# Sparse attention followed by an MLP on one core: two pairs of heads interleaved over all 128 partitions in each load of q or k

## The chip, the cores and the metric

One core of a Trainium2 chip runs the whole kernel. The metric is device time in microseconds (us); a kernel's figure is the median of its runs. Ratios are the mean time of one kernel's fast runs over that of the other's fast runs of the same rounds, so they are not quite the ratio of the medians quoted beside them. Jobs ran on different chips (the last two on the same one), so across jobs I compare the ratios to the kernel before, which ran in every job.

PE is TensorE's matmul side, DVE is VectorE, ACT is ScalarE, POOL is GpSimd, SP is the queue that issues most transfers. PSUM is the memory that PE writes its results to. "The rings", a word of the record, means here the DMA engines taken together.

## The reference

```python
batch, n_heads, seq, head_dim = 8, 8, 576, 64
scores = scale * np.matmul(q, k.transpose(0, 1, 3, 2))
mask_local = (rel >= 0) & (rel < 32)                   # heads 0 to 3
mask_strided = (rel >= 0) & (pos_k % 32 == pos_q % 32) # heads 4 to 7
attn = softmax(np.where(mask, scores, -1e9))           # cut
x = np.matmul(attn, v)                                 # -> (4608, 512)
h = x @ w_in                                           # (512, 2048)
g = np.maximum(h, 0) + alpha * np.minimum(h, 0)
return g @ w_out                                       # (2048, 512)
```

## The kernel before

Attention works on pairs of heads; two pairs of one kind (local or strided) of one batch make a half batch. A half batch is loaded, cast to fp16, transposed on PE through PSUM into `qpad` and `kT`, scored in blocks, masked, multiplied with v, and turned into columns of `xT`. The MLP runs in chunks of 512 tokens: lin1 (`hps`) and lin2 (`ops`). The first chunk, lin1(0), needs batch 0's attention; lin1(1) follows batch 1's and the first steps of batch 2's.

The loads of q and k: q on partitions 0 to 63, k on 64 to 127.

```python
st = spool.tile([128, 2304], F32, tag="qk", name="stqk")
for src, r0 in ((q, 0), (k, 64)):
    keep((k_eng if r0 and k_eng else nc.sync).dma_start(
        st[r0 : r0 + 64, 0:2048].rearrange("p (h e) -> p h e", h=4),
        src[b, h0 : h0 + 4, 0:512, :].rearrange("h (p t) d -> p h (t d)", t=8)))
# ... two more transfers for tokens 512 to 575 (the tail); v local in five, v strided in two
```

A transpose then holds q and k of one pair, and DVE copies out of PSUM:

```python
for t in range(8):
    keep(nc.tensor.transpose(tp[:, t, :], src[:, P.pr, 128 * t : 128 * t + 128], ident))
keep(nc.tensor.transpose(tt[:, 0:128], src[:, P.pr, 1024:1152], ident))
# ... ACT copies kT, DVE copies qpad, one head at a time
```

The start, in the parts that the argument touches:

```python
cast_part(0, False, "v", 0, "pool")
load_w(0, False)                     # w_in, a quarter; issued by POOL, cast on the way
cast_part(0, False, "v", 1, "pool")
load_w(1, False); load_w(2, False); load_w(3, False)   # three lines in the source
# ... batch 0's attention; SP then reads a few elements of w_in ("gate"), which holds
#     batch 1's loads back until the first half of w_in is there
for m in range(16):
    lin1_piece(0, m, True)
    if m == 8:
        # ... casts of batch 1's local part on POOL, loads of batch 2's
        for c in range(4):
            load_w(c, True)          # w_out
    attn_n(0 if m < 12 else 1, end1)
```

The softmax here doesn't subtract the row's maximum and nothing guards it: scores larger than these inputs give would overflow.

## Time and profile before

| | before |
|---|---|
| time, median of 4 runs | 370.15 us |
| lin1(0) starts | 35.5 us |
| lin1(1) starts | 84.9 us |
| rest, lin1(1) to the end | 281.4 us, PE idle 5.4 |

The prediction prints the slices, the table of stages, the chain through the hole and two stretches of the loads, and says how each is read. The rate at which loads came in is on the page too, in the same 40 slices of 9.2 us:

```profile
GB/s 158 207 148 236 235 210 198 209 210 204 215 218 222 137 168 136 135 139 155 97 161 114 167 115 30 30 30 30 30 30 30 29 59 29 29 57 32 29 59 86
```

From the second slice to the 13th it lies between 198 and 236, but for the third (148), in which POOL had not issued most of the weights yet (46 GB/s from 22 to 24 us).

### The profile page before, as it was taken

The page shows a single profiled execution, that of the slowest core. Times are in us where ns is not written, and L with a number is a line of the kernel's source. Part 1 is how long each engine was busy: PE and PEld are TensorE (multiplying, and loading weights), DVE is VectorE, ACT ScalarE, POOL GpSimd, SP SyncE. Part 2 cuts the span into 40 slices and gives each one's busy share as a digit, 9 for nine tenths or more (in the row PEclk, how much of TensorE's full clock was granted, in tenths as well). Part 3 has the DMA queues.
Part 4 walks back from the last instruction along what each step waited for, and adds up shares of the span by engine and source line. Part 5 has one row for each costly group of instructions (what it writes and reads, how often), then busy time and mean ns, then how long its engine had stood idle before and what let it go on. Part 6 is the DMA issues. An engine that isn't in the chain of part 4 may idle for free.

```text
span 366.5 us, 6531 instructions
## 1 busy us (share of the span) xinstructions
PE 330.8 (90%) x2449; PEld 185.4 (51%) x2449; DVE 219.4 (60%) x487; ACT 182.4 (50%) x360; POOL 137.7 (38%) x174
## 2 busy tenths in 40 slices
PE   5837985708999899999999999999999999999996
PEld 1525444604555455555557777555555444444444
DVE  2658589905886167757775776677667444444410
ACT  1614565504755355666665666566665444443421
POOL 2260482155478266546554654565242000000000
PEclk9876799556999999999999999999999999999999
DMA  7999999999999665567384740000000010010012
GB/s 158 207 148 236 235 210 198 209 210 204 215 218 222 137 168 136 135 139 155 97 161 114 167 115 30 30 30 30 30 30 30 29 59 29 29 57 32 29 59 86
DMA packets 54944, 44.11 MB, mean 120 GB/s; under 512 B 35696, under 2 KB 40192, under 8 KB 54912
## 3 DMA queue, kind: packets, MB, share of 16 engines
q1 hardware_dynamic: 49504, 37.24, 46.1%
q0 software_dynamic: 4512, 5.24, 8.0%
q10 hardware_dynamic: 896, 1.21, 1.7%
q8 instruction: 19, 0.31, 0.4%
q14 instruction: 13, 0.11, 0.1%
HBM read 38.43 MB, written 9.44 MB: 131 GB/s over the span
## 4 chain that ended last, share of the span: by engine, by line
PE 75%; DMA 12%; SPq 8%; POOL 2%; ACT 1%; issue 1%; DVE 0%; POOLq 0%; ACTq 0%
PE ops L456 33%; PE hps L411 31%; DMA stv<-in_v_dram 9%; SPq L130 5%; PE sp L229 3%; PE pv L258 3%; PE tp L202 3%; DMA stqk<-in_k_dram 2%; PE xp L275 2%; DMA win<-in_moe_w_in_dram 1%; SPq L103 1%; SPq L107 1%; PE ops L447 1%; ACT osb L461 1%; POOL qk L145 1%
## 5 line engine op out<-in xcount | busy, mean ns | idle before, releaser
L411 PE MATMUL hps<-xT,win 128*128 128x512 f16 (+1 forms) x640 | 148.9, 365 | 0.0
L456 PE MATMUL ops<-wout,gT 128*128 128x512 f16 x560 | 141.4, 379 | 2.0 <-ACT osb L461 2.0
L424 DVE SCALAR_TENSOR_TENSOR gT<-neg,oma,hps 128x512 f16<-128x512 f32 x144 | 106.9, 743 | 59.3 <-ACT neg L421 57.0
L421 ACT ACTIVATE neg<-hps 128x512 f32<-128x512 f32 x144 | 86.0, 597 | 83.0 <-PE hps L411 81.3
L411 PEld LDWEIGHTS <-win 128*128 128x128 f16 x640 | 60.5, 99 | 49.1 <-issue 5.5
L244 POOL TENSOR_TENSOR et<-et,masks 128x384 f16<-128x384 f16 (+2 forms) x60 | 54.4, 908 | 81.5 <-ACT et L237 80.5
L456 PEld LDWEIGHTS <-gT 128*128 128x128 f16 x560 | 50.0, 98 | 49.0 <-issue 2.8
L237 ACT ACTIVATE et<-sp 128x384 f16<-128x384 f32 (+2 forms) x96 | 45.6, 491 | 29.9 <-PE sp L229 29.9
L145 POOL CAST qk<-stqk 128x1024 f16<-128x1024 f32 (+1 forms) x44 | 34.3, 817 | 32.3 <-DMA stqk<-in_k_dram 32.3
L267 DVE TENSOR_TENSOR x<-pv,rc 72x384 f16<-72x384 f32 (+2 forms) x80 | 42.2, 527 | 2.8
L258 PEld LDWEIGHTS <-et 72*128 72x128 f16 (+1 forms) x448 | 24.8, 100 | 28.0 <-POOL et L240 8.1
L265 DVE RECIPROCAL rc<-pv 72x6 f32<-72x6 f32 (+2 forms) x80 | 14.9, 186 | 38.1 <-PE pv L258 37.8
L229 PE MATMUL sp<-qpad,kT 128*128 128x144 f16 (+1 forms) x224 | 32.6, 244 | 4.9 <-DVE qpad L212 2.4
L229 PEld LDWEIGHTS <-kT 128*128 128x128 f16 x224 | 20.6, 101 | 22.9 <-issue 3.5
L461 ACT COPY osb<-ops 128x512 f32<-128x512 f32 x35 | 20.5, 585 | 18.5 <-PE ops L456 18.3
L212 DVE COPY qpad<-tp 64x512 f16<-64x512 f16 x32 | 22.0, 688 | 7.3 <-ACT kT L212 7.1
L202 PE MATMUL tp<-ident,qk 128*128 128x128 f16 x256 | 21.6, 233 | 3.3 <-DVE qk L143 3.0
L202 PEld LDWEIGHTS <-qk 128*128 128x128 f16 x256 | 18.1, 105 | 10.1 <-DVE qk L143 3.9
L258 PE MATMUL pv<-vl,et 128*128 128x65 f16 x192 | 12.2, 195 | 11.8 <-POOL et L240 7.8
L209 DVE COPY qpad<-tp 64x512 f16<-64x512 f16 x32 | 13.5, 421 | 13.7 <-ACT kT L209 13.5
L209 ACT COPY kT<-tp 128x512 f16<-128x512 f16 x16 | 9.3, 583 | 19.3 <-PE tp L202 19.0
L258 PE MATMUL pv<-vs,et 72*128 72x65 f16 x256 | 16.6, 198 | 2.3 <-ACT et L237 1.1
(42 smaller groups left out, 179.2 us busy)
## 6 DMA issues: line engine op xcount, KB each, us to landing
out_dram<-osb SPq DMA_DIRECT2D x35, 256.0 KB, 2.0
stqk<-in_q_dram SPq DMA_DIRECT2D x16, 512.0 KB, 6.3
stqk<-in_k_dram SPq DMA_DIRECT2D x12, 512.0 KB, 7.8
stv<-in_v_dram SPq DMA_DIRECT2D x32, 160.0 KB, 4.4
stv<-in_v_dram SPq DMA_DIRECT2D x8, 512.0 KB, 5.5
win<-in_moe_w_in_dram POOLq DMA_DIRECT2D x4, 512.0 KB, 6.7
wout<-in_moe_w_out_dram POOLq DMA_DIRECT2D x4, 512.0 KB, 16.5
stqk<-in_k_dram ACTq DMA_DIRECT2D x2, 512.0 KB, 7.9
```

Of the source, the lines that this page charges most:

```text
L145: keep(nc.gpsimd.tensor_copy(o, i))
L202: keep(nc.tensor.transpose(tp[:, t, :], src[:, P.pr, 128 * t : 128 * t + 128], ident))
L229: keep(nc.tensor.matmul(sp[:, 2 * w * x : 2 * w * x + 2 * w], P.kT[:, k0 : k0 + 128], P.qpad[:, :, w * t : w * t + w], start=(x == 0), sto ...
L237: keep(nc.scalar.activation(et[0:r, 0:n], sp[0:r, 0:n], AF.Exp, scale=SCALE))
L244: keep(eng.tensor_tensor(ev, ev, m.unsqueeze(1).to_broadcast([r, n // w, w]), op=ALU.mult))
L258: keep(nc.tensor.matmul(pv[:, 65 * x : 65 * x + 65], et[0:r, c : c + 128], v16[0:r, t, 2 * P.pr + hh, :], start=(x == 0), stop=(x == nb - ...
L267: keep(nc.vector.tensor_tensor(P.x16[0:w, c0 : c0 + 64 * nb].rearrange("r (c e) -> r c e", e=64), pvv[:, :, 0:64], rc[0:w, 0:nb].unsqueeze ...
L411: keep(nc.tensor.matmul(hps[:, dst : dst + w], win16[:, kk, 128 * m : 128 * m + 128], xT[:, kk, src : src + w], start=(kk == 0 and x == 0) ...
L421: keep(nc.scalar.activation(neg, hps, AF.Relu, scale=-1.0))
L424: keep(nc.vector.scalar_tensor_tensor(gTs[n][:, m, :], neg, oma[:, m : m + 1], hps, op0=ALU.mult, op1=ALU.add))
L456: keep(nc.tensor.matmul(ops, gTs[n][:, kf, 128 * mt : 128 * mt + 128], wout16[:, kf, :], start=(kf == 0), stop=(kf == 15)))
L461: keep(nc.scalar.copy(osb, ops))
```

## The change

Its intent is to make each load of q and of k span all 128 partitions, to halve the number of transfers, and to keep PE's work the same. Partition 2p+a holds token group p of pair a, so one transpose serves both pairs and its output has the pairs interleaved. With it, `qpad` and `kT` go from three buffers of one pair to two buffers of two pairs.

```diff
-        st = spool.tile([128, 2304], F32, tag="qk", name="stqk")
+        for nm, src, eng in (("q", q, nc.sync), ("k", k, k_eng or nc.sync)):
+            st = spool.tile([128, 2, 512], F32, tag="qk", bufs=6, name=f"st{nm}")
+            base = src[b, h0 : h0 + 1, 0:1, :]
+            keep(eng.dma_start(st, bass.AP(
+                tensor=base.tensor, offset=base.offset,
+                ap=[[8 * D, 64], [2 * S * D, 2], [S * D, 2], [1, 8 * D]])))
... tails of all eight heads in two transfers per batch; v local in one, v strided in one
-    def transpose_piece(P):
+    def transpose_piece(u, nm):
+        tp = pspool.tile([128, 8, 64, 2], F16, tag="ps", name="tp")
+        for t in range(8):
+            keep(nc.tensor.transpose(
+                tp[:, t].rearrange("r p e -> r (p e)"), src[:, 128 * t : 128 * t + 128], ident))
+        main = tp.rearrange("r t p e -> r e t p" if strided else "r t p e -> r e p t")
+        if nm == "q":
+            for hh in range(2):
+                rr = slice(64 * hh, 64 * hh + 64)
+                keep(nc.vector.tensor_copy(split(qpads[u % 2][rr, :, hh, :])[0], main[rr]))
+            return
... k: two tail transposes, two copies on ACT; then the tails of q on DVE
... masks and identity in one load; the small identity of the alpha transpose no longer loaded:
         if i == 13:
+            keep(nc.vector.tensor_copy(id16, ident[0:16, 0:16]))
             keep(nc.tensor.transpose(apt[:, 0:16], alpha_r, id16))
```

More of the change, by code (lines that the diff above doesn't have):

```diff
@@ L13, with _build_consts @@
 AF = mybir.ActivationFunctionType
-def _build_masks():
+def _build_consts():
     kp = np.arange(128)[:, None]
     qf = np.arange(96)[None, :]
-    first = ((qf >= kp) & (qf < kp + 32)).astype(np.float16)
     other = ((qf + 32 >= kp) & (qf < kp)).astype(np.float16)
+    first = np.where(kp < 32, np.float16(0), other)
     ks = np.arange(128)[:, None]
@@ L26, in _build_masks @@
     mstr = ((ks % 4 == qs % 4) & (ks <= qs)).astype(np.float16)
-    return np.concatenate([first, first, other, other, mstr], axis=1)
+    ident = np.eye(128, dtype=np.float16)
+    return np.concatenate([ident, first, first, other, other, mstr], axis=1)
 @with_exitstack
@@ L49 @@
     RING = 4 * S
-    masks_dram = nc.inline_tensor(_build_masks(), name="masks").ap()
-    id_dram = nc.inline_tensor(np.eye(128, dtype=np.float16), name="ident128").ap()
-    id16_dram = nc.inline_tensor(np.eye(16, dtype=np.float32), name="ident16").ap()
+    consts_dram = nc.inline_tensor(_build_consts(), name="consts").ap()
     cpool = ctx.enter_context(tc.tile_pool(name="const", bufs=1))
     spool = ctx.enter_context(tc.tile_pool(name="stage", bufs=3))
+    tpool = ctx.enter_context(tc.tile_pool(name="tl", bufs=2))
     hpool = ctx.enter_context(tc.tile_pool(name="half", bufs=2))
@@ L72 @@
     ))
-    ident = cpool.tile([128, 128], F16)
+    consts = cpool.tile([128, 584], F16)
     id16 = cpool.tile([16, 16], F32)
-    masks = cpool.tile([128, 456], F16)
     alpha_r = cpool.tile([16, 128], F32)
     oma = cpool.tile([128, 16], F32)
-    mfirst, mother, mstr = masks[:, 0:384], masks[:, 192:288], masks[0:72, 384:456]
+    ident = consts[:, 0:128]
+    mfirst, mother, mstr = consts[:, 128:512], consts[:, 320:416], consts[0:72, 512:584]
     win16 = cpool.tile([128, 4, 2048], F16)
@@ L84 @@
     NE = 8
-    qpads = [cpool.tile([128, 2, S], F16, name=f"qpad{i}") for i in range(3)]
-    kTs = [cpool.tile([128, 640], F16, name=f"kT{i}") for i in range(3)]
+    qpads = [cpool.tile([128, 2, 2, S], F16, name=f"qpad{i}") for i in range(2)]
+    kTs = [cpool.tile([128, 2, 672], F16, name=f"kT{i}") for i in range(2)]
     vls = [cpool.tile([128, 6, 4, 65], F16, name=f"vl{i}") for i in range(2)]
@@ L89, with load_tail @@
     ets = [cpool.tile([128, 512], F16, name=f"et{i}") for i in range(NE)]
-    for t in vls + vss:
-        keep(nc.gpsimd.memset(t[:, :, :, 64:65], 1.0))
-    for t in ets:
-        keep(nc.gpsimd.memset(t[:, 288:512], 0.0))
     loaded = {}
     def load_qk(b, strided, k_eng=None):
-        st = spool.tile([128, 2304], F32, tag="qk", name="stqk")
         h0 = 4 if strided else 0
-        for src, r0 in ((q, 0), (k, 64)):
-            keep((k_eng if r0 and k_eng else nc.sync).dma_start(
-                st[r0 : r0 + 64, 0:2048].rearrange("p (h e) -> p h e", h=4),
-                src[b, h0 : h0 + 4, 0:512, :].rearrange("h (p t) d -> p h (t d)", t=8)))
-        for src, r0 in ((q, 0), (k, 64)):
-            keep(nc.sync.dma_start(
-                st[r0 : r0 + 64, 2048:2304].rearrange("p (h d) -> p h d", h=4),
-                src[b, h0 : h0 + 4, 512:576, :].rearrange("h p d -> p h d")))
-        loaded[(b, strided, "qk")] = st
+        for nm, src, eng in (("q", q, nc.sync), ("k", k, k_eng or nc.sync)):
[4 more added lines that the diff above has]
+                ap=[[8 * D, 64], [2 * S * D, 2], [S * D, 2], [1, 8 * D]])))
+            loaded[(b, strided, nm)] = st
+    def load_tail(b, eng=None):
+        st = tpool.tile([128, 512], F32, tag="tl", name="sttl")
+        for src, r0 in ((q, 0), (k, 64)):
+            keep((eng or nc.sync).dma_start(
+                st[r0 : r0 + 64, :].rearrange("p (h d) -> p h d", h=8),
+                src[b, :, 512:576, :].rearrange("h p d -> p h d")))
+        loaded[(b, "tail")] = st
     def load_v(b, strided):
@@ L114, in load_v, with win @@
         if strided:
-            for lo, hi in ((0, 64), (64, 72)):
-                keep(nc.sync.dma_start(
-                    st[lo:hi, :].rearrange("p (h e) -> p h e", h=4),
-                    v[b, 4:8, 8 * lo : 8 * hi, :].rearrange("h (p t) d -> p h (t d)", t=8)))
-        else:
-            keep(nc.sync.dma_start(
-                st[:, 0:256].rearrange("p (h d) -> p h d", h=4),
-                v[b, 0:4, 0:128, :].rearrange("h p d -> p h d")))
-            s5 = st[:, 256:1536].rearrange("p (j h d) -> p j h d", j=5, h=4)
-            for h in range(4):
-                base = v[b, h, 64:192, :]
-                win = bass.AP(
-                    tensor=base.tensor, offset=base.offset,
-                    ap=[[D, 128], [96 * D, 5], [1, D]],
-                )
-                keep(nc.sync.dma_start(s5[:, :, h, :], win))
+            keep(nc.sync.dma_start(
+                st[0:72, :].rearrange("p (h e) -> p h e", h=4),
+                v[b, 4:8, :, :].rearrange("h (p t) d -> p h (t d)", t=8)))
+        else:
+            def win(r0, n, x0, x1):
+                base = v[b, 0:1, 0:1, :]
+                off = (96 * x0 - 32 + r0) * D
+                keep(nc.sync.dma_start(
+                    st[r0 : r0 + n, 64 * x0 : 64 * x1].rearrange("p (x d) -> p x d", d=D),
+                    bass.AP(tensor=base.tensor, offset=base.offset + off,
+                            ap=[[D, n], [96 * D, x1 - x0], [1, D]])))
+            if b == 0:
+                keep(nc.gpsimd.memset(st[0:32, 0:64], 0.0))
+                win(32, 96, 0, 1)
+                win(0, 128, 1, 24)
+            else:
+                win(0, 128, 0, 24)
         loaded[(b, strided, "v")] = st
@@ L137, in load_part @@
             load_qk(b, strided)
+            if not strided:
+                load_tail(b)
     def cast_copy(eng, o, i):
@@ L159, in cast_part @@
             else:
-                i = st[:, 0:1536].rearrange("p (j h d) -> p j h d", j=6, h=4)[
-                    :, :, 2 * pr : 2 * pr + 2, :]
+                i = st[:, 768 * pr : 768 * pr + 768].rearrange(
+                    "p (h j d) -> p j h d", h=2, j=6)
             cast_copy(eng, o, i)
@@ L164, in cast_part, with cast_tail @@
         else:
-            if (b, strided, nm) not in cast16:
-                cast16[(b, strided, nm)] = hpool.tile(
-                    [128, 2, 1152], F16, tag="qk16", name="qk16")
-            t16 = cast16[(b, strided, nm)]
-            if pr == 0:
-                cast_copy("pool", t16[:, :, 1024:1152],
-                          st[:, 2048:2304].rearrange("p (a c) -> p a c", a=2))
+            t16 = hpool.tile([128, 1024], F16, tag=f"{nm}16", name=f"{nm}16")
+            cast16[(b, strided, nm)] = t16
             cast_copy(
                 eng,
-                t16[:, pr, 0:1024].rearrange("p (t h d) -> p t h d", t=8, h=2),
-                st[:, 1024 * pr : 1024 * pr + 1024].rearrange("p (h t d) -> p t h d", h=2, t=8),
-            )
+                t16.rearrange("p (t f d) -> p t f d", t=8, f=2),
+                st.rearrange("p f (t d) -> p t f d", t=8),
+            )
+    def cast_tail(b, eng):
+        t16 = tpool.tile([128, 512], F16, tag="tl16", name="tl16")
+        cast_copy(eng, t16, loaded[(b, "tail")])
+        cast16[(b, "tail")] = t16
     class Pair:
@@ L189, in make_pair @@
         P.n, P.w = (8, 72) if P.strided else (6, 96)
-        P.qpad, P.kT = qpads[g % 3], kTs[g % 3]
+        u = g // 2
+        P.qpad, P.kT = qpads[u % 2][:, g % 2], kTs[u % 2][:, g % 2]
         P.sgroups = ([0, 1, 2], [3, 4, 5], [6, 7]) if P.strided else ([0, 1], [2, 3], [4, 5])
@@ L195, in make_pair, with split, tail @@
         return P
-    def transpose_piece(P):
-        src = cast16[(P.b, P.strided, "qk")]
-        tp = pspool.tile([128, 8, 128], F16, tag="ps", name="tp")
-        tt = pspool.tile([128, 1024], F16, tag="ps", name="tt")
-        for t in range(8):
-            keep(nc.tensor.transpose(tp[:, t, :], src[:, P.pr, 128 * t : 128 * t + 128], ident))
-        keep(nc.tensor.transpose(tt[:, 0:128], src[:, P.pr, 1024:1152], ident))
-        def move(copy, o, r0, r1, c0):
-            main, tail = tp[r0:r1, :, c0 : c0 + 64], tt[r0:r1, c0 : c0 + 64]
-            if P.strided:
-                ov = o.rearrange("r (t p) -> r t p", t=8)
-                keep(copy(ov[:, :, 0:64], main))
-                keep(copy(ov[:, :, 64:72], tail.rearrange("r (p t) -> r t p", t=8)))
-            else:
-                keep(copy(o[:, 0:512].rearrange("r (p t) -> r p t", t=8),
-                          main.rearrange("r t p -> r p t")))
-                keep(copy(o[:, 512:576], tail))
-        move(nc.scalar.copy, P.kT[:, 0:576], 0, 128, 64)
+    def transpose_piece(u, nm):
+        b, strided = u // 2, u % 2 == 1
+        src = cast16[(b, strided, nm)]
+        tp = pspool.tile([128, 8, 64, 2], F16, tag="ps", name="tp")
[3 more added lines that the diff above has]
+        main = tp.rearrange("r t p e -> r e t p" if strided else "r t p e -> r e p t")
+        def split(o):
+            if strided:
+                ov = o.rearrange("r e (t p) -> r e t p", t=8)
+                return ov[:, :, :, 0:64], ov[:, :, :, 64:72]
+            return o[:, :, 0:512].rearrange("r e (p t) -> r e p t", t=8), o[:, :, 512:576]
+        if nm == "q":
[3 more added lines that the diff above has]
+            return
+        tt = pspool.tile([128, 1024], F16, tag="ps", name="tt")
+        for e in range(2):
+            c0 = 128 * (2 * int(strided) + e)
+            keep(nc.tensor.transpose(
+                tt[:, 128 * e : 128 * e + 128], cast16[(b, "tail")][:, c0 : c0 + 128], ident))
+        def tail(r0, r1, c0):
+            v = tt[r0:r1, 0:256].rearrange("r (e c) -> r e c", e=2)[:, :, c0 : c0 + 64]
+            return v.rearrange("r e (p t) -> r e t p", t=8) if strided else v
+        ko = split(kTs[u % 2][:, :, 32:608])
+        keep(nc.scalar.copy(ko[0], main))
+        keep(nc.scalar.copy(ko[1], tail(0, 128, 64)))
@@ L217, in transpose_piece @@
         for hh in range(2):
-            r0 = 64 * hh
-            move(nc.vector.tensor_copy, P.qpad[r0 : r0 + 64, hh, :], r0, r0 + 64, 0)
+            rr = slice(64 * hh, 64 * hh + 64)
+            keep(nc.vector.tensor_copy(
+                split(qpads[u % 2][rr, :, hh, :])[1], tail(rr.start, rr.stop, 0)))
     def score_piece(P, i):
@@ L227, in score_piece @@
         for x, t in enumerate(grp):
-            k0 = 72 * t if P.strided else max(0, 96 * t - 32)
+            k0 = 32 + 72 * t if P.strided else 96 * t
             keep(nc.tensor.matmul(
@@ L290, in feed, with T @@
         pieces.append((g, fn))
-    def T(g):
-        return lambda: transpose_piece(pairs[g])
+    def T(u, nm):
+        return lambda: transpose_piece(u, nm)
     def Sc(g, i):
@@ L302, in X @@
         return lambda: x_piece(pairs[g])
-    for g in (2, 3):
-        feed(T(g), 0)
+    feed(T(1, "q"), 0)
+    feed(T(1, "k"), 0)
     for g in (2, 3):
@@ L312 @@
             feed(Pv(g, i), 0)
-    for g in (0, 1):
-        feed(T(g), 0)
+    feed(T(0, "q"), 0)
+    feed(T(0, "k"), 0)
     feed(X(2), 0)
@@ L335, in plan_casts @@
         b, strided = u // 2, u % 2 == 1
-        names = (("qk", 0), ("qk", 1)) if g % 2 == 1 else (("v", 0), ("v", 1))
+        names = (("q", 0), ("k", 1)) if g % 2 == 1 else (("v", 0), ("v", 1))
         return [(b, strided, nm, pr) for nm, pr in names]
@@ L342 @@
         okP = 4 <= p < npair
-        okT = 4 <= t < npair
+        okT = 4 <= t < npair and t % 2 == 0
         okX = 4 <= x < npair
@@ L351 @@
         if okT:
-            seq.append(("T", T(t), t))
+            seq.append(("T", T(t // 2, "q"), t))
         if okX:
@@ L358 @@
             seq.append(("P", Pv(p, 1), p))
+        if okT:
+            seq.append(("T", T(t // 2, "k"), t))
         if okA:
@@ L363 @@
         todo = plan_casts(g)
-        nslots = [i for i, s in enumerate(seq) if s[0] != "S"]
+        nslots = [i for i, s in enumerate(seq) if s[0] != "S"] or list(range(len(seq)))
         for i, (kind, fn, gg) in enumerate(seq):
             extra = []
-            if todo and (kind != "S"):
+            if todo and i in nslots:
                 left = len([z for z in nslots if z >= i])
@@ L374, in run @@
                 for b, strided, nm, pr in extra:
+                    if nm == "q" and not strided:
+                        cast_tail(b, "pool")
                     cast_part(b, strided, nm, pr, "pool")
@@ L484 @@
     load_qk(0, True, nc.scalar)
-    keep(nc.scalar.dma_start(ident, id_dram))
+    keep(nc.sync.dma_start(consts, consts_dram))
+    load_tail(0, nc.gpsimd)
+    keep(nc.gpsimd.dma_start(alpha_r, moe_alpha.rearrange("(kf p) -> kf p", p=128)))
+    for t in vls + vss:
+        keep(nc.gpsimd.memset(t[:, :, :, 64:65], 1.0))
+    for t in ets:
+        keep(nc.gpsimd.memset(t[:, 288:512], 0.0))
     load_v(0, True)
@@ L488 @@
     load_v(0, False)
-    keep(nc.scalar.dma_start(masks, masks_dram))
-    keep(nc.scalar.dma_start(id16, id16_dram))
-    keep(nc.scalar.dma_start(alpha_r, moe_alpha.rearrange("(kf p) -> kf p", p=128)))
-    for i in range(3):
-        keep(nc.vector.memset(qpads[i][64:128, 0, :], 0.0))
-        keep(nc.vector.memset(qpads[i][0:64, 1, :], 0.0))
-        keep(nc.vector.memset(kTs[i][:, 576:640], 0.0))
+    for i in range(2):
+        keep(nc.vector.memset(qpads[i][64:128, :, 0, :], 0.0))
+        keep(nc.vector.memset(qpads[i][0:64, :, 1, :], 0.0))
+        keep(nc.vector.memset(kTs[i][:, :, 0:32], 0.0))
+        keep(nc.vector.memset(kTs[i][:, :, 608:672], 0.0))
     warm(12)
-    cast_part(0, True, "qk", 0, "dve")
-    cast_part(0, True, "qk", 1, "act")
+    cast_part(0, True, "q", 0, "dve")
+    cast_part(0, True, "k", 0, "act")
+    cast_tail(0, "pool")
     cast_part(0, True, "v", 0, "pool")
@@ L510 @@
         if i == 8:
-            cast_part(0, False, "qk", 0, "dve")
-            cast_part(0, False, "qk", 1, "act")
+            cast_part(0, False, "q", 0, "dve")
+            cast_part(0, False, "k", 0, "act")
         attn_step(end0)
@@ L526 @@
         load_qk(1, strided, nc.gpsimd)
+        if not strided:
+            load_tail(1)
         load_v(1, strided)
@@ L539 @@
         if m == 8:
-            for nm in ("qk", "v"):
-                for pr in range(2):
-                    cast_part(1, False, nm, pr, "pool")
-                load_part(2, False, nm)
+            cast_tail(1, "pool")
+            cast_part(1, False, "q", 0, "pool")
+            cast_part(1, False, "k", 0, "pool")
+            load_part(2, False, "qk")
+            for pr in range(2):
+                cast_part(1, False, "v", pr, "pool")
+            load_part(2, False, "v")
             for c in range(4):
```

## The prediction

> **What bounds the kernel now.** I read the page first (shares, then the 40 slices), then the table of stages, the chain that ended last in order of time, and the waits.
>
> ```profile
> PE   5837985708999899999999999999999999999996
> PEld 1525444604555455555557777555555444444444
> DVE  2658589905886167757775776677667444444410
> ...
> PEclk9876799556999999999999999999999999999999
> DMA  7999999999999665567384740000000010010012
> ```
>
> Each digit is 9.2 us of the 366.5. PE is full from the tenth slice to the end; before that it has holes (5, 3, 7, 5, 7, 0) while DMA is at 9 in slices 2 to 13. So there are two kernels here: a head limited by loads and waits, and a long body limited by TensorE. The table of stages (cut where the chain changes) puts sizes on them; the columns are length, busy time of PE, weight load, DVE, ACT, POOL, then granted clock, DMA share and GB/s:
>
> ```profile
> 0.00:35.50 35.50, 22.70 (x181) 13.24 (x182) 21.02 (x62) 11.98 (x25) 11.42 (x28) 0.83 1.02 184
> 35.50:49.50 14.00, 13.98 (x58) 5.80 (x56) 8.92 (x13) 7.17 (x13) 7.41 (x11) 0.82 1.18 232
> 49.50:73.00 23.50, 16.02 (x178) 11.63 (x175) 22.07 (x61) 14.01 (x33) 8.44 (x9) 0.82 1.15 205
> 73.00:85.10 12.10, 2.11 (x24) 1.92 (x25) 1.39 (x5) 0.83 (x3) 7.86 (x9) 0.50 1.13 206
> 85.10:366.50 281.40, 276.03 (x2016) 152.81 (x2013) 166.01 (x348) 148.39 (x290) 102.56 (x118) 0.99 0.40 96
> ```
>
> Row 1: batch 0's loads and attention, ended by the first matmul of lin1(0) (hps of the first 512 tokens). Row 2: lin1(0), PE alone. Row 3: batch 1's attention, where DVE is busy 22.07 of 23.50 us. Row 4: a hole, PE busy 2.11 of 12.10 us. Row 5: 281.4 us with only 5.4 us of PE idle. A shorter kernel must therefore bring the start of lin1(1), now at 85.1 us, forward. Most of what happens after that hides behind PE. The hole in order of time, from the chain (start, us, what):
>
> ```profile
> 65.36 3.09 SPq L103
> ...
> 70.03 6.99 DMA stqk<-in_k_dram
> ...
> 77.52 1.98 POOL qk L145 x2
> ...
> 79.58 0.62 POOL et L240
> ...
> 80.44 2.03 POOL vs L145 x2
> 82.47 0.88 POOL et L244
> ...
> 83.39 0.29 PE pv L258 x2
> 83.68 0.85 PE tp L202 x8
> ```
>
> A k load lands at 77.0; POOL, which works in order, casts behind it and only then masks the batch-2 scores that PE waits for (7.8 us of "PE pv <- POOL et" in the waits). The first row is another hole of this kind: the waits have 5.1 us of "PE tt <- POOL qk", the tail's transpose waiting from 21.8 to 26.6 for a cast queued on POOL behind v casts and weight issues.
>
> [...] Where only the SP queue runs q then k (each on 64 partitions) the rate is 213; where q on the low half runs beside k from another queue on the high half it is 305 (last column):
>
> ```profile
> 34.00:38.00 4.00, 3.44 (x15) 1.30 (x14) 1.91 (x5) 0.38 (x1) 0.00 (x0) 0.50 1.06 305
> 74.00:76.00 2.00, 0.00 (x0) 0.00 (x0) 0.00 (x0) 0.00 (x0) 0.00 (x0) 0.50 1.16 213
> ```
>
> In the packet records a 2 KB packet of such a load takes some 160 to 170 ns around 76 to 80 us, and one of a 128-partition output store late in the kernel 84 ns. [...] the qpad copy of 64x512 with contiguous reads takes 421 ns, the one that permutes takes 688.
>
> **The change, part by part.**
>
> q and k loads. Bytes and 2 KB packets stay; each transfer now spans all 128 partitions. A half batch of q and k is 1.05 MB: at 210 GB/s 5.0 us, at the 305 seen with both halves 3.4. Gain 1.6 to 1.9 us where q and k went in turn, about 0.5 to 1 where they already overlapped on two queues (batch 0, batch 1). Six halves land before the end of the hole: about 1 each for the two of batch 0, 0.7 each for batch 1, 1.8 each for batch 2: 7 us of DMA time. DMA is the bound there, so this counts.
>
> Tails and v. Tails: four small transfers per batch become two, same 256 B packets. Local v: five transfers become one (two in batch 0), same 3,072 packets. SP issues fall from 15 to 8 per batch at 0.6 us[...]. Estimate 0 to 1 us. [...]
>
> Transposes. "Serve two pairs at once" saves no TensorE instruction: per two pairs it was 2 x (8 + 1) = 18, and is 8 (q) + 8 (k) + 2 (tail) = 18. PE's body is unchanged.
>
> PSUM copies on DVE. Per two pairs, local: 4 x (688 + 180) = 3.47 us before. After: two of 1024 elements (688 + 512 x 1.06 = 1231, slope from 213 at 64 to 688 at 512) and two tails of 128 (about 215): 2.89. Strided: 4 x (421 + 213) = 2.54 before; the interleaved columns make the read step 2[...]: 2 x 1231 + 2 x 281 = 3.02. Together 6.01 becomes 5.91: nothing. The DVE-bound third row keeps its 23 us.
>
> PSUM copies on ACT: per two pairs 2 x (583 + 223) = 1.61 becomes about 0.99 + 0.27 = 1.27; 16 x 0.34 = 5.4 us, off the path.
>
> POOL. Same casts of q and k; tail cast once per batch (16 x 414 ns becomes about 8 x 625) and early, so it no longer blocks PE in the first row (5 us of wait goes). Window masks the same; one shape less on L240.
>
> Sum along the head. Batch 0's q/k land about 1 to 2 us earlier; v about 3, so POOL issues the weights about 2.5 us earlier; the tt wait goes. I re-timed the first row through T, masks, PV, X with the durations above and get lin1(0) at about 29 instead of 35.5. Then 14 us of lin1(0) and 23 of batch 1's attention bring PE to the hole at 66 to 67 instead of 73. The batch-2 strided q/k then lands at 77.0 - 2.5 (weights earlier) - 1.4 (batch 1) - 3.6 (batch 2) = 69.5; POOL needs about 2.1 us of casts, 0.9 mask, 2.0 cast and 0.9 mask as before; PE's T and X 1.7. So lin1(1) starts at about 76, some 9.5 us earlier, and the body follows unchanged: 370.1 - 9.5 = 360.6 us.
>
> **Rivals.** (a) The transfers are hidden anyway: true after 85 us (DMA share 0.40 and PE idle 5.4), false before it; the hole is behind a load. If only the first row gained and the weights' traffic kept the rest at its time, about 367. (b) DVE takes over: in the third row it is at 94%. If the step-2 copies cost more than my slope (each of the two serial per q tile), that row grows by 1 to 2 us and scores wait on qpad: about 363. (c) POOL order remains the wait: a cast that waits for a load still stands ahead of masks; gain then follows the load only, about 5: 365. (d) Loads get so early that the hole vanishes, lin1(1) at 70: 355. (e) Body pays back: bursts of transposes hold PSUM buffers while DVE copies 2.5 us per q tile; against it, lin pieces of 0.86 us stand between attention pieces and hide it. One or two us at most.
>
> **Range and chances.** The sum says 360.5 us; (d) gives the low end, (a) and (c) the high one: 353 to 367.5. 2% is 362.9, only 2.3 us above my figure, so faster by over 2% gets 0.63, within 2% 0.35, slower 0.02 (nothing lengthens the PE-bound body by 7 us).
>
> **What the profile would show.** Right: q/k-only stretches near 300 GB/s, 2 KB packets near 105 ns; no tt wait near 22 us; lin1(0) near 29 and lin1(1) near 76; about 281 us after that; PE matmul count nearly the same; qpad copies near 1.23 us. Wrong: packets still at 165 ns[...], lin1(1) still near 85 with PE waiting on another load (the weights or local v, which the change doesn't speed up), or PE idle in the body well above 5.4 us.

The sum comes to 69.5 us for the last k, 9.5 us at lin1(1) and 370.1 - 9.5 = 360.6 us. Its rates (210, 305 GB/s) and copies (421, 688 ns) are read from the trace before; that the strided copy takes 1,231 ns like the local one is an estimate from the 688 ns of the copy that permutes. The 0 to 1 us for fewer issues is the estimate: four issues of local v took 2.29 us from 16.08, 8.52 from 32.49, 16.64 from 48.62 and 7.83 from 77.55, the last with no weights under way (w_out's last packet is seen at 68.3).

## The result, and the profile after

The changed kernel takes 365.25 us (364.4 to 366.16, 4 runs) against 370.15: ratio 0.9865, interval 0.9833 to 0.9897. That is 4.9 us, inside the range given and about half of the 9.5 us expected. The likelier outcome by the prediction's own chances, faster by over 2% (0.63), did not come; within 2% had 0.35.

The page of the changed kernel, the two rows of slices that answer to those of before:

```profile
PE   6658974649998999999999999999999999999996
DMA  7989999999936083519352820000000010010012
GB/s 210 218 134 287 199 238 196 275 206 280 232 103 203 32 232 96 175 42 246 96 175 53 242 63 32 29 32 29 31 32 29 29 60 29 29 60 29 29 61 87
```

The head is one slice shorter, the loads end earlier, and slices of 230 to 290 GB/s now stand between others that are still at 200. The stages, cut at the same events as before (length, then busy PE, weight load, DVE, ACT, POOL, then granted clock, DMA share, GB/s):

```profile
0.00:32.20 32.20, 20.85 (x181) 13.43 (x182) 23.07 (x55) 11.59 (x21) 13.80 (x31) 0.89 0.91 195
32.20:45.20 13.00, 12.99 (x55) 5.52 (x55) 8.81 (x13) 7.17 (x12) 4.25 (x6) 0.87 1.04 245
45.20:70.90 25.70, 16.20 (x179) 12.39 (x176) 23.97 (x49) 12.83 (x26) 12.50 (x14) 0.78 1.14 235
70.90:79.50 8.60, 2.17 (x25) 1.82 (x24) 1.80 (x6) 0.64 (x2) 6.50 (x7) 0.50 1.18 232
79.50:363.00 283.50, 277.48 (x2017) 152.66 (x2014) 168.84 (x304) 145.39 (x268) 101.69 (x114) 0.99 0.33 94
```

The first stage lost 3.3 us (35.5 to 32.2), the hole 3.5 (12.1 to 8.6). Row 2 ends both times behind the same 52 matmuls of lin1(0), which took 13.0 us instead of 13.9, at a granted clock of 0.87 instead of 0.82; row 3 is 2.2 us longer. Rows 2 and 3 together: 37.5 us before, 38.7 after. The last row is 2.1 us longer. The hole is still there, and the chain of waits (start, us, what) shows who ends it:

```profile
44.42 13.93 DMA sttl<-in_k_dram
...
61.31 3.18 SPq L100
...
65.29 9.59 DMA stv<-in_v_dram
...
74.94 2.04 POOL vs L151 x2
76.97 0.88 POOL et L266
...
77.90 0.29 PE pv L280 x2
...
79.52 9.71 PE hps L437 x36
```

A transfer of 128 KB, batch 2's k tail, stands here with 13.9 us from issue to landing. POOL's casts behind it end at 61.3, then SP gets to issue the next loads, and the last ones land at 74.9. The rates in three stretches say why the wider loads did not shorten this more:

```profile
18.00:20.00 2.00, 0.52 (x5) 0.21 (x5) 1.90 (x7) 0.00 (x0) 2.00 (x3) 1.00 0.00 0
52.00:60.00 8.00, 3.56 (x56) 2.83 (x56) 7.11 (x15) 3.11 (x7) 1.65 (x3) 0.96 1.22 196
66.00:68.00 2.00, 0.95 (x9) 0.74 (x9) 1.89 (x8) 1.08 (x3) 1.33 (x2) 0.50 0.91 341
```

At 66 us, with q and k alone on the rings, the rate is 341 GB/s: the wide loads do what was expected. At 18 us the DMA engines stand idle. From 52 to 60 us, w_out (issued at 45.0 us, its first packet seen at 50.1) shares the rings with the 256 B packets of tails and local v. The packet records of these 8 us hold 1,228 packets of 256 B and 1,221 of 1,024 B: one for one, so the small ones move at 39 GB/s (1,228 x 256 B / 8 us) and w_out at 156; from 38 to 40 us, with hardly anything beside them, the small ones moved at 209.

### The profile page after: what moved, and what is told of

Same layout as the page of the kernel before. It is cut to its first block, busy times and chain, and to the rows that moved or that the text cites. A ratio compares the mean times of both kernels' runs of the same rounds, so it can differ in the third digit from the quotient of the medians.

```text
span 363.0 us, 6353 instructions
## 1 busy us (share of the span) xinstructions
PE 329.7 (91%) x2449; PEld 185.8 (51%) x2449; DVE 226.5 (62%) x423; ACT 177.6 (49%) x328; POOL 138.7 (38%) x170
## 4 chain that ended last, share of the span: by engine, by line
PE 81%; DMA 9%; DVE 3%; ACT 2%; POOL 2%; issue 2%; SPq 1%; POOLq 0%; ACTq 0%
PE hps L437 34%; PE ops L482 34%; DMA sttl<-in_k_dram 6%; PE sp L251 4%; PE tp L210 3%; PE pv L280 3%; DMA stv<-in_v_dram 3%; PE xp L297 2%; SPq L100 1%; PE ops L473 1%; DVE et L266 1%; DVE x L289 1%; ACT osb L487 1%; POOL vs L151 1%; ACT et L259 0%
## 5 line engine op out<-in xcount | busy, mean ns | idle before, releaser
L266 POOL TENSOR_TENSOR et<-et,consts 128x384 f16<-128x384 f16 (+2 forms) x60 | 54.2, 908 | 85.4 <-ACT et L259 84.5
L223 DVE COPY qpad<-tp 64x1024 f16<-64x1024 f16 x32 | 39.0, 1220 | 3.8 <-PE tp L210 3.5
L251 PE MATMUL sp<-qpad,kT 128*128 128x144 f16 (+1 forms) x224 | 32.8, 248 | 7.2 <-DVE qpad L240 3.8
L287 DVE RECIPROCAL rc<-pv 72x6 f32<-72x6 f32 (+2 forms) x80 | 14.8, 186 | 37.5 <-PE pv L280 37.3
L280 PEld LDWEIGHTS <-et 72*128 72x128 f16 (+1 forms) x448 | 25.6, 102 | 23.7 <-POOL et L262 3.7
L236 ACT COPY kT<-tp 128x1024 f16<-128x1024 f16 x16 | 16.2, 1011 | 20.0 <-PE tp L210 20.0
L280 PE MATMUL pv<-vl,et 128*128 128x65 f16 x192 | 12.4, 201 | 8.1 <-POOL et L262 3.4
L151 POOL CAST vs<-stv 72x1024 f16<-72x1024 f32 x16 | 16.9, 1084 | 2.9 <-DMA stv<-in_v_dram 2.9
L297 PE MATMUL xp<-consts,x 72*128 72x72 f16 (+1 forms) x224 | 15.3, 211 | 2.0 <-DVE x L289 1.7
L297 PEld LDWEIGHTS <-x 72*128 72x128 f16 (+1 forms) x224 | 12.8, 104 | 7.2 <-DVE x L289 2.4
L151 POOL CAST tl<-sttl 128x512 f16<-128x512 f32 x8 | 4.9, 618 | 28.6 <-DMA sttl<-in_k_dram 28.6
```

The lines of the kernel that those rows point to most:

```text
L151: keep(nc.gpsimd.tensor_copy(o, i))
L223: keep(nc.vector.tensor_copy(split(qpads[u % 2][rr, :, hh, :])[0], main[rr]))
L251: keep(nc.tensor.matmul(sp[:, 2 * w * x : 2 * w * x + 2 * w], P.kT[:, k0 : k0 + 128], P.qpad[:, :, w * t : w * t + w], start=(x == 0), sto ...
L266: keep(eng.tensor_tensor(ev, ev, m.unsqueeze(1).to_broadcast([r, n // w, w]), op=ALU.mult))
L280: keep(nc.tensor.matmul(pv[:, 65 * x : 65 * x + 65], et[0:r, c : c + 128], v16[0:r, t, 2 * P.pr + hh, :], start=(x == 0), stop=(x == nb - ...
L297: keep(nc.tensor.transpose(xp[:, P.w * t : P.w * t + P.w], P.x16[0 : P.w, 128 * t : 128 * t + 128], ident[0 : P.w, 0 : P.w]))
```

## The experiments

Theory W: the hole is set by loads, but by the stretch in which w_out and small packets share the rings, and by idle DMA before it; wide q and k shorten neither. Rivals: DVE's copies for two pairs at once (B); the number of transfers rather than their width; first-row gains that simply add up (F).

Starts of lin1(0) and lin1(1) are read from PE's timeline of each profiled run.

| run | median us | ratio to before, interval | lin1(0) | lin1(1) |
|---|---|---|---|---|
| changed kernel | 365.25 | 0.9865 (0.9833, 0.9897) | 32.2 | 79.3 |
| e1_id_early | 363.42 | 0.9856 (0.9823, 0.9888) | 31.1 | 78.8 |
| e2_half_part | 376.11 | 1.0201 (1.0173, 1.023) | 35.8 | 91.2 |
| e3_half_free | 367.09 | 0.9971 (0.9935, 1.0007) | 32.8 | 79.2 |
| e4_wout_late | 360.92 | 0.9803 (0.9746, 0.9859) | 32.7 | 73.6 |
| e5_before_wl | 367.13 | 0.992 (0.9865, 0.9975) | 34.9 | 77.6 |
| e6_wl_qact | 375.75 | 1.0175 (1.013, 1.0219) | 34.0 | 76.7 |
| e7_wl_id | 358.02 | 0.9689 (0.9646, 0.9733) | 30.9 | 71.7 |
| e8_qact | 378.21 | 1.0249 (1.0189, 1.0309) | 34.3 | 78.7 |
| e9_win_early | 360.3 | 0.9743 (0.9682, 0.9803) | 32.1 | 77.0 |
| e10_dup | 370.09 | 1.0 (0.9927, 1.0072) | 32.6 | 76.4 |
| e11_vsplit | 364.19 | 0.9856 (0.9789, 0.9922) | 31.3 | 76.7 |
| e12_all | 359.42 | 0.9741 (0.9715, 0.9768) | 30.8 | 71.0 |

e1 to e4 shared one job, e5 to e8 another, e9 to e11 a third, e12 a fourth.

The starts come from one profile of each. The 52 matmuls at the head of lin1(0) alone take from 12.7 us (e4) to 14.3 (e9) in these profiles, at granted clocks of 0.90 to 0.80, so a difference of a microsecond or two at lin1(1) is not sure by itself; the ratios rest on four runs or more.

### Is it the width? Cut by partitions (e2) against cut along the free dimension (e3)

```diff
 # e2
+            for z in range(2):
+                keep(eng.dma_start(st[64 * z : 64 * z + 64], bass.AP(
+                    tensor=base.tensor, offset=base.offset + z * 32 * 8 * D,
+                    ap=[[8 * D, 32], [2 * S * D, 2], [S * D, 2], [1, 8 * D]])))
 # e3
+            for z in range(2):
+                keep(eng.dma_start(st[:, z : z + 1, :], bass.AP(
+                    tensor=base.tensor, offset=base.offset + z * S * D,
+                    ap=[[8 * D, 64], [2 * S * D, 2], [S * D, 1], [1, 8 * D]])))
```

> The changed kernel with each q and each k load cut in two transfers of 64 partitions, lower half then upper half; same layout, same 2 KB packets. [...] 2 KB load packets go back from about 104 ns to 150 to 165 ns, lin1(1) starts 2 to 4 us later, time 367 to 369. Rival (the gain comes from fewer transfers or from the casts' new order): no more than 1 us slower, and as slow as the cut along the free dimension.

> Control for the one above: each q and k load cut in two transfers too, but along the free dimension, so each still spans 128 partitions. [...] packets stay near 104 ns, time within 1 us of the changed kernel (365 to 366). Rival (number of transfers counts): as slow as the cut by partitions, 367 to 369.

In both, the first figures are those of the theory that the width of a load sets the time of its packets; 104 ns is the mean of all 2 KB packets in the changed kernel's trace. Both issue the same number of transfers and move the same 2 KB packets into the same places; only the partitions that one transfer spans differ. In one job they took 376.11 and 367.09 us. The mean 2 KB packet in the first 122 us took 158.8 ns when cut by partitions and 114.5 when not (154.1 before the change, 110.6 after). A stretch of each with q and k nearly alone (e2, then e3):

```profile
52.00:58.00 6.00, 3.13 (x34) 2.02 (x32) 5.90 (x10) 2.70 (x7) 6.00 (x8) 1.00 1.07 197
```

```profile
66.00:70.00 4.00, 1.84 (x22) 1.52 (x22) 3.79 (x12) 0.88 (x2) 2.00 (x3) 0.55 0.86 271
```

With the DMA share at 1.07, e2 moves 197 GB/s; e3 moves 271 at a share of 0.86. So the width is what speeds the loads: shown. Two expectations were off. e2 is slower than even the kernel before. A reason, argued and not shown: before, q and k of batches 0 and 1 came on two queues and covered both halves at once (237 GB/s from 8 to 12 us), while in e2 both queues begin with the lower half. And e3's ratio is 1.1% above the changed kernel's, outside its expected 1 us, though its profile, of the fastest of its four runs, has lin1(1) at the same place. That is some 4 us, most of what the change gained, so the rival that the number of transfers counts for the time is not ruled out. A difference between chips explains it less well: e1, in the same job, kept 0.9856. It stays open.

### Is the hole the weights? w_out later, with the change (e4) and without (e5)

```diff
-            for c in range(4):
-                load_w(c, True)
 ...
         lin1_piece(1, m, True)
+        if m == 0:
+            for c in range(4):
+                load_w(c, True)
```

> The changed kernel with the four w_out loads issued at the first piece of lin1(1) instead of the ninth of lin1(0). Theory W (256 B packets of batch 2's tail and local v share the DMA rings one for one with the weights' packets from 50 to 63 us): the tail lands by about 50 instead of 58.4 us, batch 2's loads land 8 to 10 us earlier, the hole of 70.9 to 79.5 shrinks to 1 to 3 us, lin1(1) starts at 71 to 73 us, time 358 to 360, unless lin2(0) then waits for w_out near 92 us (that would give back some us). Rival D (DVE and ACT chains of batch 1 and POOL order set it): lin1(1) no earlier than 77, time 363 or more.

> The kernel before with w_out loaded at the first piece of lin1(1) instead of the ninth of lin1(0). Theory W says the old hole too was mainly a matter of small packets sharing the rings with the weights: then batch 2's loads land some 8 us earlier, lin1(1) starts at 77 to 79 us instead of 85, time 362 to 364.5, and the change on top of it (360.9 measured with the same edit) is worth only 2 to 4 us. Rival P (half-width loads were the whole hole): lin1(1) after 82 us, time 367 or more.

With the change, lin1(1) moves from 79.3 to 73.6 us and the ratio from 0.9865 to 0.9803. The stages of e4 from lin1(0) on:

```profile
32.65:45.20 12.55, 12.52 (x53) 5.30 (x52) 8.68 (x13) 7.17 (x12) 4.26 (x6) 0.90 1.10 270
45.20:73.55 28.35, 18.06 (x201) 14.33 (x200) 25.11 (x54) 13.45 (x27) 15.68 (x17) 0.75 1.10 236
73.55:357.50 283.95, 277.13 (x2020) 152.72 (x2017) 168.98 (x304) 145.38 (x268) 104.77 (x118) 0.99 0.36 98
```

The middle row, which is attention and hole together, shrank from 34.3 (25.7 + 8.6) to 28.35 us, and DVE is busy 25.1 us of it. Theory W is shown for the start: sharing the rings with w_out cost 5.8 us at lin1(1). Two more pairs in the table that differ in w_out (and in where the identity of the next section is cast) agree: 78.8 to 71.7 (e1, e7) and 77.0 to 71.0 (e9, e12). In time, e4's interval overlaps the changed kernel's. The start was at 73.6 and not at the 71 to 73 expected, because POOL still casts v (2.0 us) ahead of a mask that PE waits for (1.4 us), and the time was some 1 us above what was expected.

In the kernel before, the same edit moves lin1(1) by more, from 84.9 to 77.6, but the time only by 0.8%, about what e4 gains on the changed kernel (0.6%). The gain was given back later: from lin1(1) on, e5 takes 288.6 us instead of 281.4. The last of w_out's packets is seen at 105.6 us (95.8 in e4), and PE waits 3.2 us for it in lin2(0); the rest is PE busy 3.9 us longer, at a granted clock of 0.98 against 0.99 (the profiled run is the slowest of its four). So lin1(1) is where theory W put it, and the time, 367.13, missed the expected 362 to 364.5 and lies where rival P had it. That the wide loads are what makes room for a later w_out is not shown.

### First-row gains: the small identity (e1, e7) and the first weights (e9)

In PE's timeline the first row of the changed kernel has an idle time that the kernel before did not have:

```profile
21.72 0.20 PE L551 MATMUL apt<-id,alpha_r 16*128 16x16 f32 x1 [2.84 <-issue]
21.86 1.03 PE L210 MATMUL tp<-consts,q 128*128 128x128 f16 x8
```

The alpha transpose now takes its identity from a cast on DVE, which stands behind batch 0's normalisations there and runs at 21.4 us; in PE's order the transposes of batch 0's local half come next, and start at 21.86 us. It is a wait that came in place of the one removed: before, the tail's transpose waited 4.8 us for POOL at nearly the same spot.

```diff
-            keep(nc.vector.tensor_copy(id16, ident[0:16, 0:16]))
 # e1: right after the first q cast;  e7: behind the first copies (i == 1), and w_out late
+            keep(nc.vector.tensor_copy(id16, ident[0:16, 0:16]))
```

> The changed kernel with one edit: the 16x16 identity is cast right after the first q cast instead of behind batch 0's normalisations on DVE. Theory W (the loads of batch 2, slowed by the second weight load, set when lin1(1) starts): PE's 2.8 us idle ahead of the alpha transpose at 18.9 us goes, lin1(0) starts at 29 to 30 us instead of 32.2, but lin1(1) still starts at 78.5 to 79.5 us, and the time stays within 1.5 us of the changed kernel (363.8 to 365.5). Rival F (first-row gains add up): lin1(1) at 76.5, time 362 to 362.8.

> The changed kernel with w_out late and the 16x16 identity cast right after batch 0's first copies (behind them on DVE, ahead of the normalisations). PE's 2.8 us idle before the alpha transpose goes and nothing at the start moves, so lin1(0) starts at 29.5 to 30.2 us. With the loads no longer the bound this reaches lin1(1): 71 to 72 us and 358 to 359.5. If the loads still bind: 360.5 to 361.5.

In e1 the constants land later (PE's first transposes wait 2.61 us for them, 1.70 in the changed kernel) and the granted clock from 10 to 12 us is 0.50 instead of 1.00; the first strided scores start at 14.0 us instead of 12.5, and lin1(0) gains 1.1 us where 2 to 3 were expected. lin1(1) gains 0.5 and the ratio stays at 0.9856, as W says. But this profile does not show that the hole absorbed the gain: e1's lin1(0) took 14.0 us for its 52 matmuls instead of 13.0, at a granted clock of 0.81 instead of 0.87, so PE left it at 45.1 us against 45.2. In e7, with w_out late, a repair of the same kind gives 1.8 us at lin1(0) and 1.9 at lin1(1) against e4, and the ratio falls to 0.9689: 3.1% below the kernel before. Time and lin1(1) are as expected; lin1(0), at 30.9, is 0.7 us later than expected. So rival F was not borne out in e1, and in e7, with the loads out of the way, the gain of the first row reaches lin1(1).

e9 leaves w_out where it was and issues w_in ahead of the v casts on POOL, so that the DMA engines don't idle:

```diff
+    load_w(0, False)
+    load_w(1, False)
+    load_w(2, False)
+    load_w(3, False)
     cast_part(0, False, "v", 0, "pool")
-    load_w(0, False)
     cast_part(0, False, "v", 1, "pool")
-    load_w(1, False)
-    load_w(2, False)
-    load_w(3, False)
```

> The changed kernel with the four w_in loads issued on POOL ahead of the two casts of batch 0's local v, so that they no longer wait for that v to land. Theory G (the time that the wider loads gain at the front is lost again, because the DMA engines stand idle from 17 to 20.5 us until POOL issues the weights): w_in starts 2 to 3 us earlier, the gate that holds batch 1's loads opens near 26 instead of 28.6 us, batch 1's tail is cast at 38 to 39 instead of 41, lin1(1) starts at 76.5 to 77.5 instead of 79.3 us, time 362 to 363.5. Rival (the front doesn't matter to the hole): lin1(1) at 79 or later, 364.5 to 366.

```profile
16.00:18.00 2.00, 1.33 (x19) 0.85 (x19) 1.94 (x6) 0.12 (x1) 2.00 (x3) 1.00 0.61 115
18.00:20.00 2.00, 0.52 (x5) 0.21 (x5) 1.90 (x7) 0.00 (x0) 2.00 (x4) 1.00 0.98 150
```

The stretch from 18 to 20 us, at share 0.00 in the changed kernel, is at 0.98. Batch 1's tail is cast at 36.5 us instead of 41.0, lin1(1) starts at 77.0, and the ratio is 0.9743 (360.3 us, below the 362 to 363.5 expected). lin1(0) does not move (32.1), so this works through the loads alone. The gain in time is larger than lin1(1)'s 2.3 us explains; the rest I cannot place. The ratio's interval is clear of the changed kernel's; the 2.3 us by themselves are within what profiles differ by.

### The copies on DVE (e6, e8, e10)

e6 (with w_out late) and e8 (without) put the second of each two q copies on ACT.

```diff
-                keep(nc.vector.tensor_copy(split(qpads[u % 2][rr, :, hh, :])[0], main[rr]))
+                copy = nc.scalar.copy if hh else nc.vector.tensor_copy
+                keep(copy(split(qpads[u % 2][rr, :, hh, :])[0], main[rr]))
```

> The changed kernel with w_out late and with the second half of each q copy (64x1024) on ACT instead of DVE. Theory B (with the hole gone, DVE's two copies of 1.22 us in a row for two pairs set batch 1's attention, as in PE's 3.8 us wait for qpad before the strided scores): that wait shrinks by 1.2 us or more, the stretch from T(2) to lin1(1) shortens by 1.5 to 3 us, time 357.5 to 359.5. Rival (ACT's exp and kT chain sets it): no change, 360.5 to 361.5.

> The changed kernel with only the second half of each q copy on ACT, w_out early as in it. Theory W: the DVE burst is hidden by the hole, so lin1(1) stays at 78.5 to 79.5 us, batch 1's stretch ends 1.5 to 3 us earlier but the hole grows by as much, and the time is within 1 us of the changed kernel (364.2 to 366.2). Rival B' (the DVE burst is what cost the 4.6 us missing from the prediction): 361 to 363.

Both are far slower than expected under any theory. The waits of e6 tell why (in total, times, longest):

```profile
ACT qpad L224 <- DVE qpad L224: 42.2, 16, 7.7
```

ACT's copy waited for DVE's every time, 2.6 us on average, and all that ACT does behind it waited too: PE's waits for ACT's copy of lin2's result grew from 2.0 us to 10.5 in e6 and e8 alike. In the trace the ACT copy carries one semaphore wait, on the counter that DVE's copy raises, and starts 34 or 35 ns after that copy ends, all 16 times: the program itself orders the two, though they write different partitions. Why it was built so was not looked into. So these two runs made a new wait and say nothing on theory B. e10 asks the same by doubling the cost: e7 with the first copy made twice, 16 x 1.22 us more on DVE.

```diff
+                for _ in range(2 - hh):
+                    keep(nc.vector.tensor_copy(split(qpads[u % 2][rr, :, hh, :])[0], main[rr]))
```

> The run with w_out late and the early identity (358.0), with the first of the two q copies of each pair of pairs made twice on DVE: 1.22 us more in 16 places. Theory B (once the loads are out of the way, DVE's burst of copies sets batch 1's attention, where two such bursts lie, and batch 0's, where two lie): lin1(1) 3 to 5 us later (75 to 76.5 instead of 71.7), and the body after it within 1 us of its 284.4, since attention there hides behind the matmuls: time 361 to 363. Rival: DVE has room everywhere: within 1 us, 357 to 359. Rival 2: the body pays for each burst: over 364.

lin1(1) moves from 71.7 to 76.4, the upper end of what theory B gave. But the rest, which I had thought would hide it, moves too (e7 first, then e10):

```profile
71.65:356.00 284.35, 277.88 (x2020) 152.85 (x2017) 169.01 (x304) 145.39 (x268) 104.80 (x118) 0.99 0.36 97
```

```profile
76.40:368.40 292.00, 279.03 (x2019) 153.04 (x2016) 181.69 (x315) 145.80 (x268) 104.76 (x118) 0.99 0.35 93
```

Of 19.5 us added to DVE, the kernel paid 12.4 between these two profiles, of which 7.7 in the last row, though DVE is busy only 182 of 292 us there. The waits of e7 and then e10 show the form that it takes:

```profile
PE hps L437 <- DVE gT L450: 0.8, 2, 0.5
```

```profile
PE hps L438 <- DVE gT L451: 5.0, 10, 0.7
```

A copy that stands ahead of gT's activation on DVE holds lin1's PSUM buffer, and PE waits some tenths each time. Of the 7.7 us another 2.2 are PE's wait for w_out, which grew from 0.5 to 2.7. Rival 2 of the expectation is the right one: bursts on DVE are not hidden in the PE-bound part.

### The v part undone (e11) and all repairs together (e12)

e11 takes local v in four transfers again (five in batch 0) and strided v as 64 and 8 rows.

```diff
-                win(0, 128, 0, 24)
+                for h in range(4):
+                    win(0, 128, 6 * h, 6 * h + 6)
 ...  and strided v in two, as before
```

> The changed kernel with the v part undone: local v rows in four transfers (five in batch 0) instead of one, strided v as 64 plus 8 rows. Theory: the same packets cross the same rings, [...]so lin1(1) stays at 79 to 80 us and the time within 1 us of the changed kernel (364.3 to 366.3). Rival (fewer issues are a good part of the gain): 367 or more. Rival k[...]: faster by over 1 us.

Rival k is that 72 rows in one transfer lose. The ratio is 0.9856 against the changed kernel's 0.9865: v in one transfer is worth nothing that these runs can see, nor does the one transfer of 72 rows cost anything that they show. Both were undone at once, so a gain of the one and a loss of the other could cancel. Its profiled run, the fastest of its four, has lin1(1) at 76.7 and not at 79 to 80, so the start of lin1(1) varies between runs by more than I allowed.

e12 is the changed kernel with w_out late, the identity early as in e7, and w_in early.

> The changed kernel with the three edits that helped together: w_out late, the 16x16 identity cast early, w_in issued ahead of batch 0's v casts. If gains simply add, the last edit's 4 to 5 us come on top of 358.0: 353 to 354.5. Theory B (with w_out late the loads no longer bind and DVE's copies and normalisations set batch 0's and batch 1's attention, so earlier loads find nothing to shorten): lin1(0) at 30 to 31 us, lin1(1) at 71 to 72 us, time 357 to 358.5. In either case it beats both kernels.

lin1(1) starts at 71.0, as in e7, and the ratio is 0.9741, no better than e7's 0.9689 (their intervals just overlap). So w_in early adds nothing once w_out is out of the way: the expectation from theory B holds for the starts, while the time was 1 us above it. Both e7 and e12 beat the kernel before and the changed one; e7 has the lower ratio.

## Why the prediction was right or wrong

**What bounds, and the width of a load: right.** PE binds from lin1(1) on, and the time moved with that start, though by less (5.6 us there, 3.5 between the profiles). Where q and k run alone they reach 341 GB/s; e2 against e3 shows that the width does it. The step reckoned with, from 210 to 305 GB/s, is confirmed in direction and about in size: 197 (e2, 256 KB a transfer) and up to 341 (512 KB). That the 305 was near is partly luck. In its stretch, 34 to 38 us, q came in 2,048 B packets but k, on POOL's queue, in 4,096 B packets; where both came in 2,048 B packets on two queues, from 8 to 12 us, the rate was 237.

**The first row, re-timed to 29 us: too large.** It is 32.2. The wait for the tail's cast near 22 us went as said, though a shorter one for it, 1.9 us, now stands at 11.2 us, before the strided half; and the diff put a new one in its place, the identity's cast behind DVE's normalisations: 2.84 us of PE idle. The step overlooked that line of the diff. e7 gets 1.8 us of it back at lin1(0) against e4.

**"7 us of DMA time ... DMA is the bound there, so this counts": the mis-sized term.** I took the gains of each half batch off the landing time as if the rest of the chain ran at its old rate and began as much earlier. The last k landed at about 72.4, where POOL's cast stops waiting, not 69.5:

```profile
72.37 1.04 POOL L151 CAST k<-stk 128x1024 f16<-128x1024 f32 x1 [2.10 <-DMA stk<-in_k_dram]
```

There is a slip in the sum as well: its terms, 69.5 + 2.1 + 0.9 + 2.0 + 0.9 + 1.7, give 77.1 and not 76, so lin1(1) would have come 8.0 us earlier and the time would have been 362.1. Part of the gain at the front was spent with idle DMA (share 0.00 from 18 to 20 us, repaired in e9), since POOL issues the weights behind a cast (which starts at 17.78 us; w_in is issued at 18.56 and its first packet seen at 20.06); batch 1's tail was cast at 40.95 us, against 41.14 for batch 1's first cast before. And later the rings are shared with w_out for 14 us (its packets are seen from 50.1 to 64.3), where wide loads have no part (e4: 5.8 us at lin1(1)). This was a rival in the text, (a), "the weights' traffic kept the rest at its time", and the outcome lies between it and the sum.

**POOL order, rival (c): right.** POOL's v cast of 2.0 us ahead of a mask still closes the hole, and its 365 us was the best of the rivals' figures. That it is met so closely is partly luck, since it reckoned with 5 us at lin1(1) and nothing given back.

**DVE: sizes right, meaning wrong.** The copy was predicted at 1,231 ns and is 1,220, and all 32, strided and local, lie between 1,205 and 1,228, where before the strided ones took 421 ns for half the elements and the local ones 688. The text's "6.01 becomes 5.91: nothing" is 48.1 us before (all qpad copies) and 47.2 after. But they stand in bursts for two pairs: PE waits 3.8 us for qpad before batch 1's strided scores, and rows 2 and 3 together grew by 1.2 us. The text's rival (b) had both, a row longer by 1 to 2 us and scores that wait for qpad.

**The body "unchanged": not quite.** It is 2.1 us longer (281.4 to 283.5), of which 1.5 is PE's busy time. Rival (e) allowed one or two. e10 shows that DVE bursts can cause this; that they caused these 2 us was not shown.

**Transfers of v: right in the time.** e11 finds neither gain nor loss from the two together.

The sum: 9.5 us expected at lin1(1), 5.6 found, 2.1 given back in the body, 3.5 in this pair of profiles and 4.9 in the medians.

## What to carry to other kernels

Before counting a faster transfer as gained time, look at what shares the rings with it and at what issues the next one: here the gain waited behind small packets that passed one for one with the weights' (1,228 and 1,221 in 8 us), and behind a cast of 2.0 us on POOL. When a change merges two small units of work into one, look at each line it puts behind other work of an engine (a 16x16 cast kept PE waiting for 2.8 us) and at the bursts it makes: DVE was busy 182 of e10's last 292 us, and PE still waited 5.0 us in that run for DVE's gT. And test a shared resource by moving the load that shares it, and read what is given back later: w_out moved late brought lin1(1) 5.8 us forward in the changed kernel and 7.3 in the one before, but the time by 0.6 and 0.8%.
